# Where weight loads are issued among the batch loads of a fused RWKV-5 attention and soft-MoE kernel

## The chip, the cores and the metric

One core of one Trainium2 chip. The metric is device microseconds (us) from one execution of the whole program; the time of a kernel is the median over its runs. Engines are named as in the profile: PE is TensorE, DVE is VectorE, ACT is ScalarE, POOL is GpSimd, SP is SyncE. A "q" behind an engine (SPq) is its queue of instructions where it issues DMAs or waits. All DMAs run on the same 16 DMA engines; the profile calls the queue that POOL feeds q0 (software_dynamic), SP's q1 and ACT's q10.

## The reference

```python
# attention: batch 4, heads 8, seq 768, head_dim 48
for t in range(S):
    kt, vt, rt = (k[:, :, t], v[:, :, t], r[:, :, t])
    cur = np.einsum('bhd,bhe->bhde', u[None] * kt, vt)
    y[:, :, t] = np.einsum('bhd,bhde->bhe', rt, state + cur)
    state = w[None, :, :, None] * state + np.einsum('bhd,bhe->bhde', kt, vt)
# soft MoE on x = y as (3072, 384): E = 8 experts of 4 slots, F = 1024
logits = x @ phi                      # (3072, 32)
d = softmax over the 3072 tokens      # exp, divided by the column sums
slot_input = (d.T @ x).reshape(E, 4, 384)
slot_out[e] = np.maximum(slot_input[e] @ w1[e], 0.0) @ w2[e]
c = softmax over the 32 slots         # exp, divided by the row sums
return c @ slot_out.reshape(32, 384)  # (3072, 384)
```

r, k, v are (4, 8, 768, 48) fp32, w and u (8, 48), w1 (8, 384, 1024), w2 (8, 1024, 384). The maxima that the reference subtracts before exp are left out in the kernel, before and after the change alike.

## The kernel before

The recurrence is done in chunks of 128 time steps: six chunks a batch, 24 in all, numbered 0 to 23, so chunks 0 to 5 are batch 0, 6 to 11 batch 1, 12 to 17 batch 2 and 18 to 23 batch 3. Within a chunk, r and k are scaled by powers of the decay w (tables W_neg and w_rep, lines 104 to 106), transposed, multiplied into a masked score matrix and applied to v; between chunks the state goes on in bf16 times wm (w to the power 128, lines 107 to 114). Each finished chunk x is transposed, multiplied by phi (`lg`, line 267), exponentiated into Lexp and summed into un_p over all 24 chunks (`disp`, line 275). Only when the last chunk is in can unsiT (line 331), the slots' input, be formed.

**Stages.** A loop over i (line 303) runs chunk i's scores and outputs, the products r, k and u of chunk i + 2 (`mults`, line 157: three POOL multiplications and a cast of v on ACT, line 170), the transposes of chunk i + 1, the copy of r for chunk i + 1 (`r_copy`, line 173, on ACT) and the MoE work of chunks i - 1 and i - 2. Instructions of an engine run in the order in which they are written: the four engines' main loops are under a manual schedule, and only the code ahead of line 149 is ordered by the framework, ACT's table work (lines 102 to 107) excepted.

**Inputs.** r, k and v of a batch lie in tiles of a pool of two buffers. Batch 0 is loaded chunk by chunk (18 DMAs on SP, line 71), each further batch by three DMAs (line 66). Batch 1 is asked for right behind batch 0; batches 2 and 3 are written in `mults` one chunk into the batch before (line 161), and since there are two buffers, SP waits there until the batch that held the buffer is used up: its last user on ACT is the r copy of the batch's last chunk, which stands behind the cast of v of the next batch's first chunk.

**Weights.** w1 and w2 of the eight experts stay in SBUF as bf16. Each is fetched and cast by one DMA of POOL's queue (`load_w`, line 139), 16 in all. The list W_AT (line 289) says behind which step i of the loop each is issued, W_ORDER in which order: w1 of expert 0, w1 of 1, w2 of 0, w1 of 2, w2 of 1 and so on, the last two w2 of experts 6 and 7. In POOL's order a fetch of step i stands right behind the three products of chunk i + 2.

**MLP and output.** `up` (line 341) and `down` (line 353) run the experts on PE with the slots' four rows, in the order up 0, up 1, down 0, up 2, ..., up 7, down 6, down 7; every expert takes 24 weight loads and products for each. so_r (line 374) is the transposed result. The output loop (line 380) makes two row blocks at a time, one scaled by DVE and one by ACT, into o_s, a pool of three buffers, and writes each pair by a DMA on SP (line 393), 12 in all.

Of the kernel before, what the change touches and what calls it, by code (L numbers as in the profile page):

```python
# [11 lines left out]
def kernel(  # L12
# [18 lines left out]
    ES = moe_phi.shape[1]  # L31
# [15 lines left out]
    G = 4  # L47
    nG = nN // G

    wts = ctx.enter_context(tc.tile_pool(name="wts", bufs=1))  # L50
    w1_all = wts.tile([P, E, nM, F], bf, name="w1_all")
    w2_all = wts.tile([P, E, nF, Dm], bf, name="w2_all")
    cst = ctx.enter_context(tc.tile_pool(name="cst", bufs=1))
# [18 lines left out]
                                  in_=src[b, :, c * C:(c + 1) * C, :].rearrange("h p d -> p h d"))  # L72

    w_rep = cst.tile([P, H * D], f32, name="w_rep")
    nc.scalar.dma_start(out=w_rep[:], in_=w.flatten().partition_broadcast(P))
    w_pd = cst.tile([P, nP], f32, name="w_pd")
    nc.vector.memset(w_pd[:], 1.0)
    for par in range(2):
        nc.scalar.dma_start(out=w_pd[par * 64:par * 64 + D, :],
                            in_=w.rearrange("(q a) d -> a d q", a=2)[par])  # L80
    u_rep = cst.tile([P, H * D], f32, name="u_rep")
    nc.scalar.dma_start(out=u_rep[:], in_=u.flatten().partition_broadcast(P))
    load_batch(0)
    phi_f = cst.tile([P, nM, ES], f32, name="phi_f")
    nc.scalar.dma_start(out=phi_f[:], in_=moe_phi.rearrange("(mo p) s -> p mo s", p=P))

    ident = cst.tile([P, P], bf, name="ident")
    make_identity(nc, ident)
    mask_ut = cst.tile([P, P], f32, name="mask_ut")
    make_upper_triangular(nc, mask_ut, val=1.0, diag=False)  # L90

    iotash = cst.tile([P, 1], mybir.dt.int32, name="iotash")
    nc.gpsimd.iota(iotash, pattern=[[0, 1]], base=-C, channel_multiplier=1)
    ishf = cst.tile([P, 1], f32, name="ishf")
    nc.vector.tensor_copy(ishf[:], iotash[:])
    ishf2 = cst.tile([P, 1], f32, name="ishf2")
    nc.vector.tensor_scalar(out=ishf2[:], in0=ishf[:], scalar1=-1.0, scalar2=-1.0,
                            op0=ALU.mult, op1=ALU.add)

    logw_pd = cst.tile([P, nP], f32, name="logw_pd")  # L100
    W_neg = cst.tile([P, H, D], f32, name="W_neg")
    with tc.manual_schedule(engines={mybir.EngineType.Activation}):
        nc.scalar.activation(out=logw_pd[:], in_=w_pd[:], func=AF.Ln)
        nc.scalar.activation(out=w_rep[:], in_=w_rep[:], func=AF.Ln)
        nc.scalar.activation(out=W_neg[:].rearrange("p h d -> p (h d)"), in_=w_rep[:], func=AF.Exp, scale=ishf[:])  # L105
        nc.scalar.activation(out=w_rep[:], in_=w_rep[:], func=AF.Exp, scale=ishf2[:])
        nc.scalar.activation(out=w_pd[:], in_=logw_pd[:], func=AF.Exp, scale=float(C))

    wm = cst.tile([P, nP, D2], f32, name="wm")
    nc.vector.memset(wm[:], 0.0)  # L110
    for par in range(2):
        ps = slice(par * 64, par * 64 + 64)
        nc.vector.tensor_copy(wm[ps, :, par * D:(par + 1) * D],
                              w_pd[ps, :, None].to_broadcast([64, nP, D]))

    W_k3 = w_rep[:].rearrange("p (h d) -> p h d", h=H)
    u3 = u_rep[:].rearrange("p (h d) -> p h d", h=H)
    phi_s = cst.tile([P, nM, ES], bf, name="phi_s")
    nc.vector.tensor_copy(phi_s[:], phi_f[:])
    ones = cst.tile([P, P], bf, name="ones")  # L120
    nc.vector.memset(ones[:], 1.0)

    NB = 3
    rr_t, kk_t = [], []
# [24 lines left out]
    with tc.tile_pool(name="wk", bufs=2) as wk, \  # L149
         tc.tile_pool(name="wk3", bufs=3) as wk3, \  # L150
         tc.tile_pool(name="wk4", bufs=4) as wk4, \
         tc.tile_pool(name="ps", bufs=1, space=bass.MemoryType.PSUM) as ps, \
         tc.manual_schedule():
        un_p = ps.tile([P, nM + 1, ES], f32, name="un_p")
        st8 = {}

# [22 lines left out]
        def diag(i):  # L179
            b, c = divmod(i, nC)  # L180
            s = st8[i]
            nc.vector.tensor_mul(s["ku"][:], s["ku"][:], s["r_p"][:])  # L182
            sd_p = ps.tile([P, nP * D2 + H], f32, name="sd_p")
            s["sd"] = sd_p
            d = sd_p[:, nP * D2:nP * D2 + H]
            nc.vector.tensor_reduce(d, s["ku"][:], axis=mybir.AxisListType.X, op=ALU.add)  # L186
            dv = wk.tile([P, H, D], bf, name="dv")
            nc.vector.tensor_mul(dv[:], s["v"][:], d[:, :, None].to_broadcast([P, H, D]))  # L188
            s["dv"] = dv

        def trans(i):
            s = st8[i]
            t_p = ps.tile([P, 2, nP, P], bf, name="t_p")
            for a, nm in enumerate(("rr", "kk")):
                for q in range(nP):
                    nc.tensor.transpose(t_p[:, a, q, :],  # L196
                                        s[nm][:, 2 * q:2 * q + 2, :].rearrange("p h d -> p (h d)"), ident[:])
            t_s = wk.tile([P, 2, nP, P], bf, name="t_s")
            nc.scalar.copy(t_s[:], t_p[:])  # L199
            s["t"] = t_s  # L200
# [98 lines left out]
        r_copy(0)  # L299
        mults(1)  # L300
        diag(0)
        trans(0)
        for i in range(nN + 3):
            if i < nN:
# [19 lines left out]
            if i >= 5 and (i - 5) % G == 0:  # L324
                lexp_t((i - 5) // G)
            for n, at in enumerate(W_AT):
                if at == i:
# [6 lines left out]
    late.close()  # L334
    soT = cst.tile([P, nM, G, ES], bf, name="soT")
    with tc.tile_pool(name="ffn", bufs=2) as ffn, \
         tc.tile_pool(name="ffn_ps", bufs=2, space=bass.MemoryType.PSUM) as ffn_ps, \
         tc.manual_schedule():
        hs = {}

        def up(e):
            h_p = ffn_ps.tile([P, nF, Spe], f32, name="h_p")
            for fi in range(nF):
                for mi in range(nM):
                    nc.tensor.matmul(h_p[:, fi, :], w1_all[:, e, mi, fi * P:(fi + 1) * P],  # L345
                                     unsiT[:, mi, e * Spe:(e + 1) * Spe],
                                     start=(fi == 0 and mi == 0), stop=(fi == nF - 1 and mi == nM - 1),
                                     skip_group_check=True)
            hT = ffn.tile([P, nF, Spe], bf, name="hT")
            nc.vector.tensor_scalar_max(out=hT[:], in0=h_p[:], scalar1=0.0)  # L350
            hs[e] = hT

        def down(e):
            so_p = ffn_ps.tile([P, nM, Spe], f32, name="so_p")
            for mi in range(nM):
                for fi in range(nF):
                    nc.tensor.matmul(so_p[:, mi, :], w2_all[:, e, fi, mi * P:(mi + 1) * P], hs[e][:, fi, :],  # L357
                                     start=(fi == 0 and mi == 0), stop=(fi == nF - 1 and mi == nM - 1),
                                     skip_group_check=True)
            nc.vector.tensor_copy(soT[:, :, :, e * Spe:(e + 1) * Spe],  # L360
                                  so_p[:, :, None, :].to_broadcast([P, nM, G, Spe]))

        up(0)
        for e in range(E):
            if e + 1 < E:
                up(e + 1)
            down(e)

        so_r = cst.tile([P, Dm], bf, name="so_r")
        sr_p = ffn_ps.tile([P, Dm], bf, name="sr_p", bufs=1)  # L370
        for mi in range(nM):
            nc.tensor.transpose(sr_p[:, mi * P:(mi + 1) * P],
                                soT[:, mi, :, :].rearrange("p g s -> p (g s)"), ident[:])
        nc.vector.tensor_copy(so_r[:], sr_p[:])

    out_ap = out.rearrange("(no p) m -> p no m", p=P)
    with tc.tile_pool(name="ob", bufs=3) as ob, \
         tc.tile_pool(name="out_ps", bufs=2, space=bass.MemoryType.PSUM) as out_ps, \
         tc.manual_schedule():
        for g in range(nG):  # L380
            for jj in range(0, G, 2):
                o_s = ob.tile([P, 2, Dm], f32, name="o_s")
                for j in (jj, jj + 1):
                    o_p = out_ps.tile([P, Dm], f32, name=f"o_p{j}")
                    nc.tensor.matmul(o_p[:], LexpT[j * ES:(j + 1) * ES, g, :], so_r[j * ES:(j + 1) * ES, :],  # L385
                                     tile_position=(j * ES, 0))
                    ni = g * G + j
                    if j % 2 == 0:
                        nc.vector.tensor_scalar_mul(o_s[:, 0, :], o_p[:], rsum_r[:, ni:ni + 1])  # L389
                    else:  # L390
                        nc.scalar.activation(out=o_s[:, 1, :], in_=o_p[:], func=AF.Copy,  # L391
                                             scale=rsum_r[:, ni:ni + 1])
                nc.sync.dma_start(out=out_ap[:, g * G + jj:g * G + jj + 2, :], in_=o_s[:])
# [30 lines left out]
```

## Time and profile before

| what | value |
|---|---|
| median of 3 runs | 164.43 us (162.64 to 167.54) |
| the profiled execution | 164.1 us |
| its span, first to last instruction | 162.3 us |
| granted clock of PE, mean over the span | 0.774 of full speed |
| busy: PE, DVE, ACT, POOL | 84.6, 93.6, 77.9, 84.5 us (52, 58, 48, 52% of the span) |
| moved by DMA | 32.13 MB, mean 198 GB/s |
| of it q0 (weights), q1 (r, k, v, output), q10 (small tables) | 12.58, 18.88, 0.44 MB |

How to read it: times are us from the span's start. A timeline's row gives start, duration, engine, line and operation, and in brackets how long the engine had been idle and what it had waited for. The page's slices cut the span into 40 equal parts of 4.06 us; a digit is a busy share in tenths. In the DMA view of a stretch the slices are those of the stretch. MB are counted at the size written, so a weight's fp32 source counts half. A fetch's "us to landing" runs from its issue to its semaphore.

### The profile page before, as it was taken

To read this page: it belongs to the slowest core of one execution; us is meant where nothing else is said; L and a number is where in the kernel's file an instruction comes from. 1 tells how busy PE (TensorE), PEld (TensorE's weight loads), DVE (VectorE), ACT (ScalarE), POOL (GpSimd) and SP (SyncE) were. 2 spreads that over 40 slices of the span, in tenths; PEclk is the share of its full clock that TensorE was granted. 3 is DMA by queue.
4 is the path that set the end of the run, shared out by engine and by line. 5 is a ranking of instruction groups with operands and counts; after the bars stand their busy time and mean duration, and the time that the engine had idled before them with its cause. 6 is when DMAs were issued, how large, how long until landed. Compare 5 with 4: busy or idle time off the path is not lost.

```text
span 162.3 us, 3621 instructions
## 1 busy us (share of the span) xinstructions
PE 84.6 (52%) x1433; PEld 63.4 (39%) x1433; DVE 93.6 (58%) x198; ACT 77.9 (48%) x163; POOL 84.5 (52%) x97
## 2 busy tenths in 40 slices
PE   0004987804789874678720000077778549974400
PEld 0003665603577653456520000065556339961100
DVE  2016889904788995999930000079999822235560
ACT  0295568307668929987500000477796420005550
POOL 2019999493869997999820091079996000000000
PEclk9999999975556999999995555559999955555555
DMA  4999997999859999999999999209999992007994
GB/s 76 197 213 210 218 258 191 253 256 183 236 161 266 257 259 181 222 243 222 221 235 230 230 246 248 53 10 168 211 184 203 164 204 39 4 4 267 346 370 182
DMA packets 48593, 32.13 MB, mean 198 GB/s; under 512 B 20160, under 2 KB 45504, under 8 KB 48576
## 3 DMA queue, kind: packets, MB, share of 16 engines
q0 software_dynamic: 11520, 12.58, 47.6%
q1 hardware_dynamic: 35952, 18.88, 42.5%
q10 hardware_dynamic: 1104, 0.44, 1.6%
q8 instruction: 11, 0.18, 0.4%
q14 instruction: 6, 0.05, 0.1%
HBM read 39.77 MB, written 4.72 MB: 274 GB/s over the span
## 4 chain that ended last, share of the span: by engine, by line
DMA 31%; SPq 21%; DVE 17%; PE 16%; ACT 8%; issue 4%; ACTq 0%; DVEq 0%
DMA v_b<-in_v_dram 23%; SPq L66 12%; SPq L71 8%; DVE at_s L213 5%; DMA out_dram<-o_s 5%; PE h_p L345 3%; PE so_p L357 3%; ACT t_s L199 3%; DVE sd_p L186 3%; PE t_p L196 3%; DVE ku L182 3%; DVE dv L188 3%; DMA w_rep<-in_w_dram 3%; DVE o_s L389 2%; ACT xt_s L264 2%
## 5 line engine op out<-in xcount | busy, mean ns | idle before, releaser
L182 DVE TENSOR_TENSOR ku<-ku,r_p 128x384 f32<-128x384 f32 x24 | 13.2, 548 | 33.7 <-ACT r_p L176 32.6
L168 POOL TENSOR_TENSOR ku<-k_b,u_rep 128x384 f32<-128x384 f32 x24 | 24.0, 1002 | 14.9 <-DVE sd_p L186 14.1
L199 ACT COPY t_s<-t_p 128x1024 bf16<-128x1024 bf16 x24 | 24.3, 1011 | 15.6 <-PE t_p L196 15.6
L166 POOL TENSOR_TENSOR kk<-k_b,w_rep 128x384 bf16<-128x384 f32 x24 | 24.1, 1003 | 13.8 <-DMA k_b<-in_k_dram 11.3
L213 DVE TENSOR_TENSOR at_s<-at_p,mask_ut 128x512 bf16<-128x512 f32 x48 | 30.7, 682 | 0.0
L165 POOL TENSOR_TENSOR rr<-r_b,W_neg 128x384 bf16<-128x384 f32 x24 | 24.2, 1008 | 10.7 <-ACT W_neg L105 10.0
L170 ACT CAST v_bf<-v_b 128x384 bf16<-128x384 f32 x24 | 12.1, 506 | 33.4 <-DMA v_b<-in_v_dram 33.4
L271 PE MATMUL xl_p<-phi_s,xt_s 128*128 128x32 bf16 x72 | 5.9, 184 | 37.5 <-ACT xt_s L264 37.3
L271 PEld LDWEIGHTS <-xt_s 128*128 128x128 bf16 x72 | 3.5, 100 | 40.1 <-ACT xt_s L264 40.1
L196 PE MATMUL t_p<-ident,rr 128*128 128x128 bf16 x96 | 11.1, 249 | 12.8 <-POOL rr L165 12.8
L391 ACT ACTIVATE o_s<-o_p,rsum_r 128x384 f32<-128x384 f32 x12 | 6.8, 581 | 19.4 <-PE o_p L385 14.7
L186 DVE TENSOR_REDUCE sd_p<-ku 128x8 f32<-128x384 f32 x24 | 13.5, 561 | 0.8
L188 DVE TENSOR_TENSOR dv<-v_bf,sd_p 128x384 bf16<-128x384 bf16 x24 | 13.3, 553 | 0.8
L249 PE MATMUL y_p<-v_bf,at_s 128*128 128x48 bf16 x192 | 12.5, 192 | 2.4 <-DVE at_s L213 2.3
L264 ACT COPY xt_s<-xl_p 128x384 bf16<-128x384 bf16 x24 | 11.5, 481 | 4.1 <-PE xl_p L262 4.0
L222 PE MATMUL y_p<-dv,ident 128*128 128x384 bf16 x24 | 9.2, 383 | 6.8 <-DVE dv L188 6.6
L196 PEld LDWEIGHTS <-rr 128*128 128x128 bf16 x96 | 6.4, 108 | 15.9 <-POOL rr L165 12.8
L253 ACT CAST x_t<-y_p 128x384 bf16<-128x384 f32 x24 | 11.6, 485 | 0.3 <-PE y_p L249 0.3
L209 PE MATMUL at_p<-t_s 64*128 64x128 bf16 x192 | 11.1, 246 | 1.2 <-ACT t_s L199 1.1
L239 DVE TENSOR_TENSOR st<-sd_p,wm 128x384 bf16<-128x384 f32 x20 | 11.0, 550 | 1.2 <-PE sd_p L235 1.1
L176 ACT COPY r_p<-r_b 128x384 f32<-128x384 f32 x24 | 11.7, 488 | 0.0
L196 PE MATMUL t_p<-ident,kk 128*128 128x128 bf16 x96 | 10.9, 246 | 0.4 <-POOL kk L166 0.4
(63 smaller groups left out, 166.8 us busy)
## 6 DMA issues: line engine op xcount, KB each, us to landing
w_all<-in_moe_w_dram POOLq DMA_DIRECT2D x16, 768.0 KB, 9.5
out_dram<-o_s SPq DMA_DIRECT2D x12, 384.0 KB, 2.4
r_b<-in_r_dram SPq DMA_DIRECT2D x6, 192.0 KB, 3.6
k_b<-in_k_dram SPq DMA_DIRECT2D x6, 192.0 KB, 3.8
v_b<-in_v_dram SPq DMA_DIRECT2D x6, 192.0 KB, 3.6
w_rep<-in_w_dram ACTq DMA_DIRECT2D x1, 192.0 KB, 4.3
u_rep<-in_u_dram ACTq DMA_DIRECT2D x1, 192.0 KB, 5.3
phi_f<-in_moe_phi_dram ACTq DMA_DIRECT2D x1, 48.0 KB, 5.9
```

Of the source, the lines that this page charges most:

```text
L66: nc.sync.dma_start(out=t[:].rearrange("p h c d -> p (h c) d")[:, :, 0:D], in_=src[b].rearrange("h (c p) d -> p (h c) d", p=C))
L71: nc.sync.dma_start(out=t[:, :, c, 0:D], in_=src[b, :, c * C:(c + 1) * C, :].rearrange("h p d -> p h d"))
L165: nc.gpsimd.tensor_mul(rr[:, :, 0:D], r_b[:, :, c, 0:D], W_neg[:])
L166: nc.gpsimd.tensor_mul(kk[:, :, 0:D], k_b[:, :, c, 0:D], W_k3)
L168: nc.gpsimd.tensor_mul(ku[:], k_b[:, :, c, 0:D], u3)
L182: nc.vector.tensor_mul(s["ku"][:], s["ku"][:], s["r_p"][:])
L186: nc.vector.tensor_reduce(d, s["ku"][:], axis=mybir.AxisListType.X, op=ALU.add)
L188: nc.vector.tensor_mul(dv[:], s["v"][:], d[:, :, None].to_broadcast([P, H, D]))
L196: nc.tensor.transpose(t_p[:, a, q, :], s[nm][:, 2 * q:2 * q + 2, :].rearrange("p h d -> p (h d)"), ident[:])
L199: nc.scalar.copy(t_s[:], t_p[:])
L213: nc.vector.tensor_mul(at_s[:, a, :, :], at_p[a][:], mask_ut[:, None, :].to_broadcast([P, nP, P]))
L264: nc.scalar.copy(xt_s[:].rearrange("p m t -> p (m t)"), xl_p[:, 0:nM * P])
```

## The change

Five things change. First, W_AT: the first weight fetch moves from step 4 to step 9, the second to 10, two more stand at step 15, and twelve follow from step 16 on, two of them at steps 16 and three at step 24. Second, the whole kernel is under one manual schedule, where before the preparation (other than ACT's) was ordered by the framework. Third, the preparation: w_rep is asked for by SP ahead of the batch loads, w_pd and phi by POOL, u_rep alone by ACT; ACT loads its Ln table on a dummy value (`warm`) and then does the decay tables with nothing between; the iota for the exponents is POOL's first instruction. Fourth, w to the power 128 is made by seven squarings on DVE (`tables()`, called behind `diag(0)`) instead of Ln and Exp on ACT, and wm and phi's cast are made there as well. Fifth, the output pool has six buffers.

```diff
+    ctx.enter_context(tc.manual_schedule())
     wts = ctx.enter_context(tc.tile_pool(name="wts", bufs=1))
...
-    nc.scalar.dma_start(out=w_rep[:], in_=w.flatten().partition_broadcast(P))
-    w_pd = cst.tile([P, nP], f32, name="w_pd")
-    nc.vector.memset(w_pd[:], 1.0)
-    for par in range(2):
-        nc.scalar.dma_start(out=w_pd[par * 64:par * 64 + D, :],
-                            in_=w.rearrange("(q a) d -> a d q", a=2)[par])
+    nc.sync.dma_start(out=w_rep[:], in_=w.flatten().partition_broadcast(P))
     u_rep = cst.tile([P, H * D], f32, name="u_rep")
     nc.scalar.dma_start(out=u_rep[:], in_=u.flatten().partition_broadcast(P))
     load_batch(0)
-    phi_f = cst.tile([P, nM, ES], f32, name="phi_f")
-    nc.scalar.dma_start(out=phi_f[:], in_=moe_phi.rearrange("(mo p) s -> p mo s", p=P))
...
+    for par in range(2):
+        nc.gpsimd.dma_start(out=w_pd[par * 64:par * 64 + D, :],
+                            in_=w.rearrange("(q a) d -> a d q", a=2)[par])
+    phi_f = cst.tile([P, nM, ES], f32, name="phi_f")
+    nc.gpsimd.dma_start(out=phi_f[:], in_=moe_phi.rearrange("(mo p) s -> p mo s", p=P))
...
-    with tc.manual_schedule(engines={mybir.EngineType.Activation}):
-        nc.scalar.activation(out=logw_pd[:], in_=w_pd[:], func=AF.Ln)
-        nc.scalar.activation(out=w_rep[:], in_=w_rep[:], func=AF.Ln)
-        nc.scalar.activation(out=W_neg[:].rearrange("p h d -> p (h d)"), in_=w_rep[:], func=AF.Exp, scale=ishf[:])
-        nc.scalar.activation(out=w_rep[:], in_=w_rep[:], func=AF.Exp, scale=ishf2[:])
-        nc.scalar.activation(out=w_pd[:], in_=logw_pd[:], func=AF.Exp, scale=float(C))
+    nc.scalar.activation(out=warm[:], in_=warm[:], func=AF.Ln)
+    nc.scalar.activation(out=w_rep[:], in_=w_rep[:], func=AF.Ln)
+    nc.scalar.activation(out=W_neg[:].rearrange("p h d -> p (h d)"), in_=w_rep[:], func=AF.Exp, scale=ishf[:])
+    nc.scalar.activation(out=w_rep[:], in_=w_rep[:], func=AF.Exp, scale=ishf2[:])
...
+    def tables():
+        for _ in range(C.bit_length() - 1):
+            nc.vector.tensor_mul(w_pd[:], w_pd[:], w_pd[:])
+        for par in range(2):
+            ps = slice(par * 64, par * 64 + 64)
+            nc.vector.tensor_copy(wm[ps, :, par * D:(par + 1) * D],
+                                  w_pd[ps, :, None].to_broadcast([64, nP, D]))
+        nc.vector.tensor_copy(phi_s[:], phi_f[:])
...
-        W_AT = [4, 7, 9, 10, 11, 12, 13, 14, 15, 16, 17, 18, 19, 20, 21, 22]
+        W_AT = [9, 10, 15, 15, 16, 16, 17, 18, 19, 20, 21, 22, 23, 24, 24, 24]
...
         diag(0)
+        tables()
         trans(0)
...
-    with tc.tile_pool(name="ob", bufs=3) as ob, \
+    with tc.tile_pool(name="ob", bufs=6) as ob, \
```

On ACT, the start of the program before. w_rep and w_pd are the decay, phi_f and u_rep other constants, v_bf the cast of chunk 0's v, r_p the copy of its r.

```order
L75 DMA w_rep<-in_w_dram 128x384
L79 DMA w_pd<-in_w_dram 48x4x1 x2
L82 DMA u_rep<-in_u_dram 128x384
L85 DMA phi_f<-in_moe_phi_dram 128x3x32
L103 ACT_TABLE_LOAD
L103 ACTIVATE logw_pd<-w_pd 128x4
L104 ACTIVATE w_rep<-w_rep 128x384
L170 CAST v_bf<-v_b 128x384
L176 COPY r_p<-r_b 128x384
L105 ACT_TABLE_LOAD
L105 ACTIVATE W_neg<-w_rep,ishf 128x384
```

The same place after the change:

```order
L78 DMA u_rep<-in_u_dram 128x384
L104 ACT_TABLE_LOAD
L104 ACTIVATE warm<-warm 128x1
L105 ACTIVATE w_rep<-w_rep 128x384
L106 ACT_TABLE_LOAD
L106 ACTIVATE W_neg<-w_rep,ishf 128x384
L107 ACTIVATE w_rep<-w_rep,ishf_102 128x384
L173 CAST v_bf<-v_b 128x384
```

Four of the five DMA issues, the Ln of w_pd and the two chunk-0 instructions between the tables have gone from ahead of W_neg.

On POOL before, from the last product of chunk 16 to the products of chunk 18, batch 3's first, with a weight fetch (w_all) behind each chunk. rr, kk and ku are the three products of a chunk.

```order
L168 TENSOR_TENSOR ku<-k_b,u_rep 128x384
L142 DMA w_all<-in_moe_w_dram 128x3x1024
L165 TENSOR_TENSOR rr_140<-r_b,W_neg 128x8x48
L166 TENSOR_TENSOR kk_142<-k_b,w_rep 128x8x48
L168 TENSOR_TENSOR ku<-k_b,u_rep 128x384
L144 DMA w_all<-in_moe_w_dram 128x8x384
L165 TENSOR_TENSOR rr_132<-r_b,W_neg 128x8x48
L166 TENSOR_TENSOR kk_134<-k_b,w_rep 128x8x48
L168 TENSOR_TENSOR ku<-k_b,u_rep 128x384
L142 DMA w_all<-in_moe_w_dram 128x3x1024
```

The same engine after the change, from the end of chunk 17's products to chunk 19's first two:

```order
L169 TENSOR_TENSOR kk_138<-k_b,w_rep 128x8x48
L171 TENSOR_TENSOR ku<-k_b,u_rep 128x384
L148 DMA w_all<-in_moe_w_dram 128x8x384
L146 DMA w_all<-in_moe_w_dram 128x3x1024
L168 TENSOR_TENSOR rr_128<-r_b,W_neg 128x8x48
L169 TENSOR_TENSOR kk_130<-k_b,w_rep 128x8x48
L171 TENSOR_TENSOR ku<-k_b,u_rep 128x384
L148 DMA w_all<-in_moe_w_dram 128x8x384
L146 DMA w_all<-in_moe_w_dram 128x3x1024
L168 TENSOR_TENSOR rr_132<-r_b,W_neg 128x8x48
L169 TENSOR_TENSOR kk_134<-k_b,w_rep 128x8x48
```

Before, nine fetches stand ahead of chunk 18's products; after, four do, the last two of them directly ahead of these products, and two more stand directly behind.

## Rows read from the trace of the kernel before

**Rows 1.** The page: DMA in 40 slices, and weight queue's packets, MB, share.

```profile
DMA  4999997999859999999999999209999992007994
...
q0 software_dynamic: 11520, 12.58, 47.6%
```

**Rows 2.** The chain of waits: start, duration, what.

```profile
75.98 27.44 DMA v_b<-in_v_dram
...
133.04 0.27 DVE unsiT L331
```

**Rows 3.** Timeline of ACT, 30 to 110 us: start, duration, [idle before <-releaser].

```profile
36.64 0.51 ACT L170 CAST v_bf<-v_b 128x384 bf16<-128x384 f32 x1 [6.68 <-DMA v_b<-in_v_dram]
...
60.53 0.51 ACT L170 CAST v_bf<-v_b 128x384 bf16<-128x384 f32 x1 [2.86 <-DMA v_b<-in_v_dram]
...
103.51 0.51 ACT L170 CAST v_bf<-v_b 128x384 bf16<-128x384 f32 x1 [23.84 <-DMA v_b<-in_v_dram]
```

**Rows 4.** Timeline of SP: start, duration, DMA issued.

```profile
19.68 0.82 SPq L66 DMA_DIRECT2D r_b<-in_r_dram  x1
...
46.48 4.25 SPq L66 DMA_DIRECT2D v_b<-in_v_dram  x1
62.47 0.70 SPq L66 DMA_DIRECT2D r_b<-in_r_dram  x1
```

**Rows 5.** Timeline of POOL: weight issues, four of sixteen and the last pair.

```profile
34.13 0.93 POOL L142 DMA_DIRECT2D w_all<-in_moe_w_dram  x1
...
55.94 0.94 POOL L144 DMA_DIRECT2D w_all<-in_moe_w_dram  x1
...
79.67 0.94 POOL L144 DMA_DIRECT2D w_all<-in_moe_w_dram  x1
...
107.59 0.94 POOL L144 DMA_DIRECT2D w_all<-in_moe_w_dram  x1
...
122.63 1.82 POOL L144 DMA_DIRECT2D w_all<-in_moe_w_dram  x2
```

**Rows 6.** DMA: 92:96 (q0, q1), 110:134 (q0), 108:137 (40 slices).

```profile
q0 software_dynamic: 610, 0.47, 74.4%
q1 hardware_dynamic: 612, 0.47, 46.8%
...
q0 software_dynamic: 4715, 4.54, 120.1%
...
GB/s 0 19 58 133 201 203 204 207 214 220 203 215 215 154 140 192 197 203 211 211 205 216 212 209 124 110 173 187 174 201 220 190 198 204 203 198 94 43 12 23
```

**Rows 7.** Stretches: us, busy time of each engine, granted clock, DMA share, GB/s.

```profile
2.00:22.00 20.00, 7.08 (x65) 4.73 (x66) 8.08 (x16) 10.79 (x18) 10.24 (x11) 1.00 1.04 204
...
103.00:109.00 6.00, 3.15 (x39) 2.62 (x39) 2.87 (x5) 4.53 (x10) 2.33 (x3) 0.50 0.03 6
```

**Rows 8.** DMA issues at 26, 46, 122.6 and 123 us: KB, us to landing.

```profile
v_b<-in_v_dram SPq DMA_DIRECT2D x1, 0.2 KB, 10.0
...
v_b<-in_v_dram SPq DMA_DIRECT2D x1, 0.2 KB, 14.0
...
w_all<-in_moe_w_dram POOLq DMA_DIRECT2D x1, 768.0 KB, 9.8
...
w_all<-in_moe_w_dram POOLq DMA_DIRECT2D x2, 768.0 KB, 11.3
```

**Rows 9.** Timeline of ACT, 0 to 12 us.

```profile
7.00 1.28 ACT L103 ACT_TABLE_LOAD   x1 [7.00 <-DMA w_pd<-in_w_dram]
...
11.06 0.61 ACT L105 ACTIVATE W_neg<-w_rep,ishf 128x384 f32<-128x384 f32 x1
```

**Rows 10.** Timelines of PE and DVE at the MLP's end; DMA in 147:160.5.

```profile
141.24 0.78 PE L357 MATMUL so_p<-hT,w_all 128*128 128x4 bf16 x24
...
143.97 0.21 DVE L360 CAST soT<-so_p 128x48 bf16<-128x48 f32 x1 [0.43 <-PE so_p L357]
...
GB/s 0 314 387 410 378 419 382 410 391 387 114 419 382 360 410 400 396 396 405 232 264 410 391 351 414 391 405 391 410 159 410 396 310 410 396 401 382 423 278 0
```

More of the change, by code (lines that the diff above doesn't have):

```diff
@@ L83 @@
     load_batch(0)
-    phi_f = cst.tile([P, nM, ES], f32, name="phi_f")
-    nc.scalar.dma_start(out=phi_f[:], in_=moe_phi.rearrange("(mo p) s -> p mo s", p=P))
[L87 to L90, printed above, removed]
+    w_pd = cst.tile([P, nP], f32, name="w_pd")
+    nc.vector.memset(w_pd[:], 1.0)
+    warm = cst.tile([P, 1], f32, name="warm")
+    nc.vector.memset(warm[:], 1.0)
     iotash = cst.tile([P, 1], mybir.dt.int32, name="iotash")
@@ L98 @@
                             op0=ALU.mult, op1=ALU.add)
-    logw_pd = cst.tile([P, nP], f32, name="logw_pd")
-    W_neg = cst.tile([P, H, D], f32, name="W_neg")
-    with tc.manual_schedule(engines={mybir.EngineType.Activation}):
-        nc.scalar.activation(out=logw_pd[:], in_=w_pd[:], func=AF.Ln)
-        nc.scalar.activation(out=w_rep[:], in_=w_rep[:], func=AF.Ln)
-        nc.scalar.activation(out=W_neg[:].rearrange("p h d -> p (h d)"), in_=w_rep[:], func=AF.Exp, scale=ishf[:])
-        nc.scalar.activation(out=w_rep[:], in_=w_rep[:], func=AF.Exp, scale=ishf2[:])
-        nc.scalar.activation(out=w_pd[:], in_=logw_pd[:], func=AF.Exp, scale=float(C))
+    ident = cst.tile([P, P], bf, name="ident")
@@ new lines @@
+    make_identity(nc, ident)
+    mask_ut = cst.tile([P, P], f32, name="mask_ut")
+    make_upper_triangular(nc, mask_ut, val=1.0, diag=False)
+    for par in range(2):
[3 more added lines that the diff above has]
+    nc.gpsimd.dma_start(out=phi_f[:], in_=moe_phi.rearrange("(mo p) s -> p mo s", p=P))
+    W_neg = cst.tile([P, H, D], f32, name="W_neg")
@@ L109 @@
+    nc.scalar.activation(out=warm[:], in_=warm[:], func=AF.Ln)
+    nc.scalar.activation(out=w_rep[:], in_=w_rep[:], func=AF.Ln)
+    nc.scalar.activation(out=W_neg[:].rearrange("p h d -> p (h d)"), in_=w_rep[:], func=AF.Exp, scale=ishf[:])
+    nc.scalar.activation(out=w_rep[:], in_=w_rep[:], func=AF.Exp, scale=ishf2[:])
     wm = cst.tile([P, nP, D2], f32, name="wm")
     nc.vector.memset(wm[:], 0.0)
[L111 to L114, printed above, removed]
+    ones = cst.tile([P, P], bf, name="ones")
@@ L116 @@
+    nc.vector.memset(ones[:], 1.0)
+    phi_s = cst.tile([P, nM, ES], bf, name="phi_s")
+    def tables():
[6 more added lines that the diff above has]
+        nc.vector.tensor_copy(phi_s[:], phi_f[:])
     W_k3 = w_rep[:].rearrange("p (h d) -> p h d", h=H)
@@ L117 @@
     u3 = u_rep[:].rearrange("p (h d) -> p h d", h=H)
[L118 to L121, printed above, removed]
     NB = 3
@@ L151 @@
          tc.tile_pool(name="wk4", bufs=4) as wk4, \
-         tc.tile_pool(name="ps", bufs=1, space=bass.MemoryType.PSUM) as ps, \
-         tc.manual_schedule():
+         tc.tile_pool(name="ps", bufs=1, space=bass.MemoryType.PSUM) as ps:
         un_p = ps.tile([P, nM + 1, ES], f32, name="un_p")
@@ L336 @@
     with tc.tile_pool(name="ffn", bufs=2) as ffn, \
-         tc.tile_pool(name="ffn_ps", bufs=2, space=bass.MemoryType.PSUM) as ffn_ps, \
-         tc.manual_schedule():
+         tc.tile_pool(name="ffn_ps", bufs=2, space=bass.MemoryType.PSUM) as ffn_ps:
         hs = {}
@@ L376 @@
     out_ap = out.rearrange("(no p) m -> p no m", p=P)
-    with tc.tile_pool(name="ob", bufs=3) as ob, \
-         tc.tile_pool(name="out_ps", bufs=2, space=bass.MemoryType.PSUM) as out_ps, \
-         tc.manual_schedule():
+    with tc.tile_pool(name="ob", bufs=6) as ob, \
+         tc.tile_pool(name="out_ps", bufs=2, space=bass.MemoryType.PSUM) as out_ps:
         for g in range(nG):
```

## Prediction

> **What bounds the kernel now.** I read the page's slices first, then the chain of waits, then the timelines of ACT, SP and POOL around the place where the chain sits longest, and last the DMA view of single stretches. The profiled run took 164.1 us, its span 162.3, so 1.8 us lie around the span; the median shown is 164.43, 0.3 above that run. The DMA line stands at 9 in most slices (4.06 us each) up to the 25th and again from 109.6 to 134, with two nearly empty slices between, from 101.4 to 109.6, and three from 133.9 to 146 [rows 1]. So up to 136 us the kernel is a stream of transfers with one hole in it; after that come the MLP's last products and a write-out of some 15 us.
>
> The chain shows where compute stands still: 27.44 us on batch 3's v [rows 2]. ACT tells the same from the waiting side: its cast of that v starts at 103.51 after 23.84 us of idle time, batch 2's at 60.53 after 2.86 [rows 3]. POOL's timeline shows why the fetch is late: seven of the sixteen weight fetches are issued from 55.94 to 79.67 [rows 5], while SP asks for batch 3 only at 62.47 [rows 4]. In 92 to 96 us the two queues moved 0.47 MB each [rows 6]: batch 3 had half of the engines. While compute stands, nothing issues weights, and from 103 to 109 us the DMA engines are busy 3% of the time [rows 7]. The attention ends with the unsiT product at 133.3 [rows 2], and the MLP follows at once, since by then nearly all weights are in. The median of the last two fetches is 11.3 us from issue to landing and the earlier one took 9.8, so the last took 12.8; issued at 123.6, one 0.9 us issue after the 122.63 of the pair, it landed at 136.4 [rows 5, 8].
>
> On this the forecast turns: removing 23.84 us of stall is not worth 23.84 us. All bytes still have to come, so what the change is worth is read from when the last weight can land.
>
> **Start and tables.** W_neg was ready at 11.67 behind a table load that had waited 7.00 us for w_pd [rows 9]; that wait goes, and POOL can begin by up to 7.0 us earlier. Worth nothing: ACT sits idle for 6.68 us before batch 1's first cast at 36.64 [rows 3], and that landing is set by transfers that run full from 2 us on (busy share 1.04 [rows 7]). Without that cover it would be worth up to 7.0 us. Added are seven squarings, two copies and a cast on DVE, and three DMA issues on POOL, each at most the 0.94 us of a weight issue [rows 5], 2.8 us together, while POOL waits for W_neg anyway. SP issues w_rep ahead of r. I take 0 for all of it, bounds -0.5 and +0.5, one DMA issue either way.
>
> **Batch 2.** Three weight issues, the first at 34.13 and the last at 55.94 [rows 5], move behind its requests. Its v took 14.0 us from issue to landing; batch 1's, with no weight beside it, 10.0 [rows 8]. Issued at 46.48 [rows 4] it lands at 56.5, before ACT asks at 57.67 (60.53 less 2.86). So the wait of 2.86 us goes, and SP's request for batch 3, which waits for a copy of r that ACT makes right behind that cast, moves from 62.47 to 59.6. Bounds: 0 to 2.86. The price is that from 36.6 to about 40 us the DMA engines now have nothing to do, where they moved the first weight.
>
> **Batch 3.** Two weights run beside it, issued where the ones of 55.94 and some four us later stood. A weight is 12.58 MB / 16 = 0.786 MB; weights alone moved 4.54 MB in the 24 us from 110 to 134 [rows 6], 189 GB/s, 4.16 us each. So these two fill 57.5 to 65.8. Batch 1 took from its first issue at 19.68 [rows 4] to 36.6, 16.9 us; batch 3 from 59.6 lands at 76.5 alone, and at 79.5 if it has half of the engines until 65.8. ACT reaches its cast at 79.67 - 2.86 = 76.8, so some 3 us of the 23.84 are left. The attention then needs what it needed from 103.51 to 133.3, 29.8 us, and ends near 109.
>
> **What is late next: the weights.** Fourteen of sixteen are still to come. Two stand behind chunk 17's products, which ended where the issue at 79.67 stands [rows 5] and now end at 76.8; the others follow at one or two a chunk, and a chunk takes under 4 us (19.1 us for the six from 60.53 to 79.67), so the queue is not empty again. A weight's data comes 1.1 to 2.5 us after its issue: 107.59 the issue, above zero from 108.7, full from 110.9 in the first row of 108 to 137 [rows 5, 6]; I take 1.6. From 78.4 then: what is left of batch 3, 1.1 us, and 14 x 4.16 = 58.2 end at 137.7; the landing shows 0.4 later (136.0 and 136.4 before), 138.1. From both sides: the best slices run at some 205 GB/s, 3.84 each, last landing 133.7; with ramp and run-out six took from 108.6 to 136.0, 4.57 each, last landing 143.9. I take 4.16, the row of weights alone over the longest stretch. POOL's issues wait until the fetch eight earlier has landed, which at 4.16 us each is the case; cost 0, and one fetch (4.2 us) if it were not.
>
> **MLP and end.** Its products now run as each weight arrives and hide under the stream. After the last landing stand 24 products (0.78 us), a DVE copy (0.21) and two hand-overs, 1.1 us in all: 139.2, where soT ended at 144.18 [rows 10]. Minus 5.0.
>
> **Write-out.** With three buffers the stream has dips: 38 of 40 slices of 0.34 us hold data, 12.8 us for twelve pairs of 384 KB (4.72 MB), though between dips it runs at some 400 GB/s [rows 10]. Six buffers put twice as many in flight; at 400 it takes 11.8. Minus 1.0, bounds 0 and -1.3.
>
> Sum: 164.1 - 5.0 - 1.0 = 158.1 against the profiled run; the median is 0.3 higher, so 158.4.
>
> **Rivals.**
> A, the gain is eaten by the weights' tail. Fourteen at 4.57 land at 143.9, soT ends at 145.0: 164.1 + 0.8 - 1.0 = 163.9. For it: in 108 to 137 us single slices fall to 110 to 154 GB/s [rows 6]. Against: most of the 4.57 is the ramp at one end and the run-out at the other, and both come once.
> B, slower: DMA time left idle early that cannot be made up. If batch 3 takes 20.9 us (batch 1's 16.9 and the 4.0 by which batch 2's v was slower [rows 8]) from an unmoved 62.47, it lands at 83.4; if the weights make no headway before that and take 4.57 after it, the last lands at 147.8, soT ends at 148.9: 164.1 + 4.7 - 0 = 168.8. It decides from a last landing of about 147. For it: 36.6 to 40 us and a gap near 56 are now given away. Against: 103 to 109, empty before [rows 7], is filled.
> The Trainium skill speaks for B: "DMA: Bandwidth & Descriptors", Rules for kernel authors, has a transfer issued early, compute laid over it, and its semaphore waited for late. By that rule alone the old order is the better; this trace speaks against it in so far as early weights took half of batch 3's engines.
> C, better: weights at 3.84, last landing 133.7, soT 134.8: 164.1 - 9.4 - 1.3 = 153.4. For it: the slices at 205; against: none of the stretches holds that rate throughout.
> D, the change doesn't do what it says: batch 2 is late all the same and the stall shrinks little. That counts only if batch 3 lands after 108, since 108 + 29.8 is the forecast's last landing; otherwise it is A or B.
>
> **How the numbers follow.** Forecast 0.70, A 0.19, B with the bad part of D 0.06, C 0.05. A measurement of this kernel can tell about 2% from no change: below 161.1 is faster, above 167.7 slower. Forecast and C lie below, 0.75; A within; B above. The range leaves out C's end, B and the upper half of A: 154.0 to 163.5.
>
> **What would show it.** Right: ACT's wait for batch 3's v falls from 23.84 us to under 8; unsiT is done near 109; the DMA slices stay at 9 from 58 us to the last weight, which lands at 136 to 140; MLP products wait for transfers; the write-out has no dips. Wrong: the last weight after 143, idle DMA slices between 80 and 135, or an attention that still ends after 130.

## The result, and the profile after

| | median us | range, runs | ratio to the kernel before |
|---|---|---|---|
| before | 165.16 | 162.64 to 167.54, 4 | |
| after | 154.58 | 154.02 to 155.14, 4 | 0.9452, 95% interval 0.9339 to 0.9566 |

The kernel is 5.5% faster (4.3 to 6.6%). Executions more than 1.5% above the fastest of their kernel are left out of the ratios and stay in the medians. The forecast was 158.4 us in a range of 154.0 to 163.5; the time is 3.8 us under the forecast, 0.6 above the lower end and 1.2 above rival C (153.4). The profiled execution took 154.98 us, its span 153.2; before it was 164.1 and 162.3. The lines of the changed kernel stand two to four higher: the cast of v is L173, the fetches L146 and L148, soT L363, the output DMA L395.

The page of the kernel after, DMA and GB/s in 40 slices, now of 3.83 us each:

```profile
DMA  3999998964389929996899999999999999907994
GB/s 65 196 216 202 220 223 254 278 198 117 98 231 285 267 58 155 205 284 186 250 297 209 207 206 208 209 209 207 209 207 208 207 210 202 171 1 278 400 399 157
```

The page of the kernel before, GB/s in slices of 4.06 us:

```profile
GB/s 76 197 213 210 218 258 191 253 256 183 236 161 266 257 259 181 222 243 222 221 235 230 230 246 248 53 10 168 211 184 203 164 204 39 4 4 267 346 370 182
```

The hole at 101 to 110 us (there the 26th and 27th slice) is gone. From the 22nd to the 34th slice the weights' stream now stands at 202 to 210 GB/s; before, from the 28th to the 33rd, it went between 164 and 211. In place of the hole are two small gaps, at the 10th and 11th slice and at the 15th. The view of stretches names them; its columns are those of [rows 7]:

```profile
37.00:40.50 3.50, 1.32 (x17) 1.09 (x18) 1.61 (x4) 3.08 (x7) 0.45 (x1) 0.54 0.07 13
54.50:57.50 3.00, 2.38 (x43) 1.77 (x44) 2.93 (x7) 2.59 (x7) 2.59 (x4) 1.00 0.02 6
82.00:132.00 50.00, 31.23 (x665) 25.78 (x665) 27.06 (x64) 19.56 (x45) 23.41 (x26) 0.67 1.23 208
```

Two gaps of some 3 us with next to no transfer (13 and 6 GB/s), then 50 us at 208 GB/s without a break.

ACT's casts of the first chunk of batches 1, 2 and 3, the answer to [rows 3]:

```profile
36.91 0.51 ACT L173 CAST v_bf<-v_b 128x384 bf16<-128x384 f32 x1 [4.31 <-DMA v_b<-in_v_dram]
...
57.83 0.50 ACT L173 CAST v_bf<-v_b 128x384 bf16<-128x384 f32 x1
...
80.90 0.51 ACT L173 CAST v_bf<-v_b 128x384 bf16<-128x384 f32 x1 [2.94 <-DMA v_b<-in_v_dram]
```

The stall of 23.84 us is now 2.94, that of 2.86 is gone. SP's requests for batch 3, its DMAs for the output, and POOL's fetches two to six and the last pair, answering to [rows 4, 5]:

```profile
60.70 0.70 SPq L67 DMA_DIRECT2D r_b<-in_r_dram  x1
61.87 8.18 SPq L67 DMA_DIRECT2D k_b<-in_k_dram  x1
70.51 4.13 SPq L67 DMA_DIRECT2D v_b<-in_v_dram  x1
138.09 9.92 SPq L395 DMA_DIRECT2D out_dram<-o_s  x12
```

```profile
59.87 0.80 POOL L146 DMA_DIRECT2D w_all<-in_moe_w_dram  x1
...
76.23 0.95 POOL L148 DMA_DIRECT2D w_all<-in_moe_w_dram  x1
77.18 0.76 POOL L146 DMA_DIRECT2D w_all<-in_moe_w_dram  x1
...
80.80 0.94 POOL L148 DMA_DIRECT2D w_all<-in_moe_w_dram  x1
81.73 0.76 POOL L146 DMA_DIRECT2D w_all<-in_moe_w_dram  x1
...
103.69 1.80 POOL L148 DMA_DIRECT2D w_all<-in_moe_w_dram  x2
```

All sixteen are issued by 105.5 us (before: 124.45), so the queue holds several fetches from 82 us on. Then the MLP's end, PE's last products and DVE's unsiT and last soT, answering to [rows 2, 10]:

```profile
127.00 0.80 PE L348 MATMUL h_p<-unsiT,w_all 128*128 128x4 bf16 x24 [2.92 <-DMA w_all<-in_moe_w_dram]
130.86 0.80 PE L360 MATMUL so_p<-hT,w_all 128*128 128x4 bf16 x24 [3.06 <-DMA w_all<-in_moe_w_dram]
134.76 0.80 PE L360 MATMUL so_p<-hT,w_all 128*128 128x4 bf16 x24 [3.10 <-DMA w_all<-in_moe_w_dram]
```

```profile
110.98 0.26 DVE L335 TENSOR_TENSOR unsiT<-un_p,csum_r 128x96 bf16<-128x96 f32 x1
...
135.60 0.21 DVE L363 CAST soT<-so_p 128x48 bf16<-128x48 f32 x1 [3.69 <-PE so_p L360]
```

The attention ends 22 us sooner (unsiT at 111.2 against 133.3), yet soT only 8.4 us sooner (135.81 against 144.18): towards the end PE does 0.80 us of products and waits 3 us for the next weight, 3.86 and 3.90 us apart. The last one is in at about 134.7. Before, the MLP ran from the attention's end to soT in 10.9 us without a wait for a weight, so there the attention set the end; now the weights do. From soT to the end of the span are 17.4 us, 18.1 before; the DMA view of 138 to 153.2 us shows the write-out without a dip:

```profile
GB/s 0 0 121 376 400 392 408 392 392 408 396 416 388 392 404 396 404 408 388 392 408 400 396 408 388 400 404 400 392 408 392 392 408 340 4 0 0 0 0 22
```

So of the profiled 9.1 us, 8.4 lie ahead of soT, which now follows the last weight's landing, and 0.7 in the write-out.

### The profile page after: what moved, and what is told of

Same layout as the page of the kernel before. It is cut to its first block, busy times and chain, and to the rows that moved or that the text cites. A ratio compares the mean times of both kernels' runs of the same rounds, so it can differ in the third digit from the quotient of the medians.

```text
span 153.2 us, 3605 instructions
## 1 busy us (share of the span) xinstructions
PE 86.6 (57%) x1433; PEld 65.3 (43%) x1433; DVE 98.2 (64%) x206; ACT 77.7 (51%) x162; POOL 86.2 (56%) x100
## 4 chain that ended last, share of the span: by engine, by line
DMA 38%; SPq 21%; POOL 12%; PE 10%; ACT 6%; DVE 4%; issue 4%; ACTq 0%; DVEq 0%; POOLq 0%
DMA w_all<-in_moe_w_dram 20%; DMA v_b<-in_v_dram 14%; SPq L72 12%; SPq L67 10%; DMA out_dram<-o_s 4%; POOL rr L168 3%; PE t_p L199 3%; POOL kk L169 2%; POOL ku L171 2%; POOL w_all L148 2%; ACT t_s L202 2%; PE at_p L212 2%; ACT xt_s L267 1%; POOL w_all L146 1%; ACT r_p L179 1%
## 5 line engine op out<-in xcount | busy, mean ns | idle before, releaser
L185 DVE TENSOR_TENSOR ku<-ku,r_p 128x384 f32<-128x384 f32 x24 | 13.1, 547 | 16.3 <-POOL ku L171 8.9
L173 ACT CAST v_bf<-v_b 128x384 bf16<-128x384 f32 x24 | 12.2, 507 | 10.5 <-DMA v_b<-in_v_dram 10.5
L252 PEld LDWEIGHTS <-at_s 128*128 128x128 bf16 x192 | 8.5, 103 | 9.5 <-DVE at_s L216 8.6
L199 PE MATMUL t_p<-ident,kk 128*128 128x128 bf16 x96 | 11.5, 254 | 0.3 <-POOL kk L169 0.3
```

Of the source, the lines that this page charges most:

```text
L199: nc.tensor.transpose(t_p[:, a, q, :], s[nm][:, 2 * q:2 * q + 2, :].rearrange("p h d -> p (h d)"), ident[:])
L252: nc.tensor.matmul(y_p[:, h * D:(h + 1) * D], s["at"][:, a, q, :], s["v"][:, h, :], start=False, stop=(a == 1 and q == nP - 1), skip_group ...
```

## Experiments

All kernels compute the whole reference. Diffs of W_AT are against the changed kernel, unless another is named; a ratio is to the kernel before, run beside it, with its 95% interval. "Stall" is ACT's wait for batch 3's v (23.84 us before, 2.94 after); soT is the start of the last one (143.97 before, 135.60 after).

### The list alone, and all but the list

w_only is the kernel before with only the new list; w_old is the changed kernel with only the old list back.

```diff
-        W_AT = [9, 10, 15, 15, 16, 16, 17, 18, 19, 20, 21, 22, 23, 24, 24, 24]
+        W_AT = [4, 7, 9, 10, 11, 12, 13, 14, 15, 16, 17, 18, 19, 20, 21, 22]
```

> The kernel before with the new list of steps for the weight fetches and nothing else. Theory (the last weight's landing sets the end, and the list alone moves it): last landing near 135, write-out still with dips, 155.3 to 156.3 us. Rival (the new preparation carries part of the gain): 157.5 us or more, with batch 1 landing later than in the changed kernel.

> The changed kernel with the old list of steps: preparation and six output buffers alone. Theory: only the write-out gains, 0.7 to 1.0 us against the kernel before, so 164 to 164.5 us, with the stall on batch 3's v back at 20 us or more. Rival (preparation or the one schedule matters): 162.5 us or less.

w_only took 156.67 us, ratio 0.9488 (0.9433 to 0.9544): stall 5.39, unsiT at 113.00, soT at 136.93. It falls between the two expectations; the list carries most of the gain. w_old took 164.58 by its median, as the theory had it, but its ratio, 0.9858 (0.9779 to 0.9936), is a gain of 2.3 us, between the theory's 0.7 to 1.0 and the rival, and leaves open whether the preparation carries part. Its profile goes with the theory: the stall is back at 20.59, soT at 144.03, and only the write-out is shorter, by 0.8 us. Its page, GB/s in 40 slices of 4.04 us, has the hole at 101 to 109 us again, and behind it, where fetches are issued one a chunk, 173 to 204 GB/s:

```profile
GB/s 73 195 211 211 207 250 267 167 283 177 178 156 291 228 293 209 247 269 215 228 234 231 228 235 232 70 14 188 196 173 176 194 204 44 4 4 200 399 400 171
```

### Three output buffers

```diff
-    with tc.tile_pool(name="ob", bufs=6) as ob, \
+    with tc.tile_pool(name="ob", bufs=3) as ob, \
```

> The changed kernel with three output buffers. Theory: the dips come back in the write-out, 0.7 to 1.0 us more than the changed kernel, 155.3 to 155.6. Rival (buffers are not what made the dips): unchanged, 154.6.

155.37 us, ratio 0.9424 (0.9351 to 0.9497). The dips of [rows 10] are back, as the DMA view of 138 to 153.2 us shows, and the twelve output issues take 12.07 us on SP instead of 9.92:

```profile
GB/s 0 307 384 396 400 404 392 396 396 162 400 392 336 412 400 400 392 239 352 416 307 404 404 352 408 408 222 408 408 311 392 396 388 392 239 0 0 0 0 22
```

From soT to the end of the span are 18.3 us, 17.4 in the kernel after: in the profiles six buffers are worth 0.9 us. In the timed runs this is not shown: the medians are 0.8 us apart, but the ratios (0.9424 and 0.9452) are the other way round, and their intervals overlap.

### Fetches into the first gap, and none before step 16

first_at_4 puts one fetch where the DMA engines stood idle at 37 us; late_all keeps every weight until batch 3 is in.

```diff
-        W_AT = [9, 10, 15, 15, 16, 16, 17, 18, 19, 20, 21, 22, 23, 24, 24, 24]
+        W_AT = [4, 9, 10, 15, 15, 16, 16, 17, 18, 19, 20, 21, 22, 23, 24, 24]     # first_at_4
+        W_AT = [16, 16, 16, 16, 17, 17, 17, 17, 18, 19, 20, 21, 22, 23, 24, 24]   # late_all
```

> The changed kernel with one fetch at step 4 again, which fills the empty stretch of the DMA engines between batch 1's landing and batch 2's data (36.8 to 40.4 us in the changed kernel's trace); each later fetch moves up one place. Theory (DMA engines idle early are paid for at the end): the last landing comes one weight, 3.8 us, earlier, 150.8 us. Rival (a fetch before batch 2 delays the batches, and that is what the list was to avoid): 154.6 us or more.

> The changed kernel with all sixteen fetches behind batch 3's first products, none between the batches. Theory (idle DMA time early is paid at the end): no stall on batch 3's v, and yet the last landing is two weights later, near 142.5, 162.5 us. Rival (what helps is that nothing runs beside the batch loads): 154.6 us or less.

first_at_4 took 151.66 us, ratio 0.9163 (0.9104 to 0.9222): stall 3.43, unsiT at 112.21 (later than after), soT at 132.48, 3.1 us sooner. late_all took 164.06, ratio 0.9994 (0.9955 to 1.0033). In it batch 3 is no longer waited for at all, unsiT is at 111.05, and nothing is gained, because soT is at 145.31. Its stretches (columns as in [rows 7]) show what was given away, 4 and 7 us with next to no transfer:

```profile
36.50:40.50 4.00, 1.11 (x15) 0.88 (x16) 1.40 (x3) 3.16 (x7) 0.24 (x1) 0.65 0.03 7
55.00:62.00 7.00, 5.62 (x96) 4.13 (x95) 6.86 (x15) 5.75 (x13) 5.91 (x7) 1.00 0.00 0
```

This is rival B's mechanism, at work once too much is moved. A stall of 23.84 us removed whole is worth 0 there. Each weight not moved early is paid at the end: the two that late_all moves no longer before batch 3 is in are 2 x 3.84 = 7.7 of the 9.7 us by which its soT is later than after's (the other 2.0 are the later start of the weights' data, 81.2 us against 79.2), and the one more of first_at_4 gave 3.1 of its 3.84.

### How many fetches are waiting

> The changed kernel with one fetch at step 15 and one at each step from 16 to 23, the last five behind step 24, so that from 78 to about 100 us one or two fetches are queued where the changed kernel has two to five. Theory (the 189 GB/s of the kernel before in 110 to 134 us came from too short a queue, the 205 of the changed kernel from fetches that wait ready): 185 to 197 GB/s in 84 to 100 us, last landing 1 to 2.5 us later, 155.5 to 157 us. Rival (the rate is what it is with one fetch running, and the pauses of before came from something else): 203 to 207 GB/s there and 154.6 us.

```diff
-        W_AT = [9, 10, 15, 15, 16, 16, 17, 18, 19, 20, 21, 22, 23, 24, 24, 24]
+        W_AT = [9, 10, 15, 16, 17, 18, 19, 20, 21, 22, 23, 24, 24, 24, 24, 24]
```

single took 158.14 us, ratio 0.9664 (0.9586 to 0.9742), soT at 137.97. The DMA view of 84 to 107 us, 40 slices, first of single (one fetch a chunk), then of the kernel after:

```profile
GB/s 214 207 214 214 235 175 126 189 196 198 200 199 213 213 200 214 199 221 207 163 154 183 176 190 199 214 157 173 182 202 207 214 203 182 128 153 167 205 188 184
DMA packets 3902, 4.40 MB, mean 191 GB/s; under 512 B 81, under 2 KB 2788, under 8 KB 3898
```

```profile
GB/s 220 210 207 214 236 184 196 197 208 202 206 207 212 216 221 203 210 219 200 195 203 203 210 200 228 197 213 212 228 199 214 212 193 203 203 212 202 201 216 208
DMA packets 4321, 4.78 MB, mean 208 GB/s; under 512 B 94, under 2 KB 3153, under 8 KB 4317
q0 software_dynamic: 4317, 4.73, 121.3%
```

The same stretch: 191 against 208 GB/s. With one fetch a chunk the stream sags to 126 to 160 again and again, as in 110 to 134 before [rows 6]; with more waiting it doesn't. The packets of q0 show where the sags stand: at the change from one fetch to the next, when the next was issued late. Of the 14 changes in single, before and w_old at which the next fetch had been issued 2.4 to 4.1 us ahead, ten fall below 165 GB/s (over 0.6 us). Of the 59 changes in these three and in after, shifted, first_at_4 and ob3 with 5.4 us or more, none falls below 175. The pace of issuing alone does not explain it: the fetches of before from 107.59 to 122.63 and those of after from 85.35 to 100.38 came 3.76 us apart alike, enough for 209 GB/s, and ran at 189 with little ahead of them and at 206 behind others (q0's row). In single it has a part: 4.11 us apart from 79.92 to 100.47, its fetches could bring no more than 191. Once its last eight are issued, single's stream too runs at 207 (110 to 132 us). The rate came as expected; soT came 2.4 us later, inside the 1 to 2.5 expected, while the medians lie 3.5 apart, more than expected.

### Filling both gaps

```diff
-        W_AT = [9, 10, 15, 15, 16, 16, 17, 18, 19, 20, 21, 22, 23, 24, 24, 24]
+        W_AT = [4, 8, 9, 10, 15, 15, 16, 16, 17, 18, 19, 20, 21, 22, 23, 24]
```

> The changed kernel with fetches at steps 4, 8, 9 and 10, two each at 15 and 16, and one a step after that. Theory (only the last landing counts, and the attention, done at 111 us, has some 20 us to spare): the stall on batch 3's v grows to 6 to 10 us, the attention ends at 115 to 119, and the time still falls below that of one fetch at step 4, to 148.5 to 150 us. Rival (more fetches between the batches take back the gain through that stall): 151.7 us or more.

A miss: 155.19 us, ratio 0.948 (0.9383 to 0.9577). The stall grew to 15.11 us, and POOL, which issues the fetches, stood at chunk 19's ku, behind which the next fetch is written:

```profile
92.62 0.51 ACT L173 CAST v_bf<-v_b 128x384 bf16<-128x384 f32 x1 [15.11 <-DMA v_b<-in_v_dram]
```

```profile
95.76 1.00 POOL L171 TENSOR_TENSOR ku<-k_b,u_rep 128x384 f32<-128x384 f32 x1 [11.76 <-DVE sd_p L189]
```

The queue ran low meanwhile (142 GB/s in the page's slice from 95.6 to 99.4 us). Three fetches instead of two ran beside batches 2 and 3. SP's issue of batch 3's k, 4.99 us long in late_all with no fetch beside it and 8.18 after, took 10.56 here and lasted until 71.97 instead of 70.05; v was asked for from 72.42 to 76.84. What goes with 2 us becoming 12 of stall is told below.

The theory left out a term: the end is the later of the last landing and the attention's end plus the MLP. unsiT was done at 122.40, PE then made the products with no wait for a weight, and soT ended at 135.47, 13.1 us on. The weights were late as well, since their last packets ended at 132.5, 1.2 us after those of first_at_4, where one fetch more ahead should bring them sooner. The time that the attention can spare is the 20 us of the expectation less the MLP.

### One fetch fewer beside the batches

```diff
-        W_AT = [9, 10, 15, 15, 16, 16, 17, 18, 19, 20, 21, 22, 23, 24, 24, 24]
+        W_AT = [4, 8, 9, 15, 15, 16, 16, 17, 18, 19, 20, 21, 22, 23, 24, 24]
```

> The changed kernel with its first three fetches at steps 4, 8 and 9, then two each at 15 and 16 and one a step. Theory (idle DMA time is paid at the end, as long as the batches land in time and the queue holds two or more): the gap near 56 us closes as well, batch 3's v lands within 3 us of where one fetch at step 4 left it, last landing near 129, 149.0 to 150.5 us. Rival (a fetch beside batch 2's end delays batch 3 and the queue runs dry behind it, as with four fetches between the batches): 151.7 us or more.

149.12 us (148.91 to 150.07, 6 runs), ratio 0.9082 (0.9052 to 0.9112), as expected, and below both kernels. Both gaps are filled, the stall is 0.65, soT at 130.68. Its stretches, columns as in [rows 7]:

```profile
37.00:40.50 3.50, 1.22 (x16) 0.99 (x17) 1.51 (x3) 3.17 (x7) 0.43 (x2) 0.71 1.07 201
54.50:57.50 3.00, 2.57 (x44) 1.95 (x44) 2.93 (x6) 2.66 (x7) 3.00 (x4) 1.00 1.12 203
```

### The preparation

no_prep is the kernel before with the new list and six buffers; after_5 is the changed kernel once more on the same chip, both in five rounds.

> The kernel before with the new list of steps and six output buffers, the preparation as it was. The changed kernel runs beside it on the same chip. Theory (the preparation is hidden behind batch 1's load): within 0.7 us of the changed kernel, 154.6 to 155.3. Rival (the preparation carries a part, as the 1.3 us between the list alone and the changed kernel with three buffers suggest): 1.0 to 1.8 us above it.

> The changed kernel as it is, for the comparison on one chip: 154.6 us by both.

no_prep took 156.45 us (154.74 to 159.92), ratio 0.9513 (0.9476 to 0.955); after_5 155.34 (154.14 to 156.89), ratio 0.9421 (0.9378 to 0.9463). The intervals just fail to meet (0.9476 and 0.9463): the preparation, the one schedule and `tables()` together, which no run separates, are worth 1.1 us by the medians and 1.5 by the ratios. no_prep's profiled execution was its fastest, with soT at 135.45, and shows no loss. no_prep_again and no_prep_third are two more profiled executions of it.

> The kernel before with the new list and six output buffers, preparation as before, profiled once more: its first profiled execution was its fastest (154.74 us against a median of 156.45), so what makes the median slower than that of the changed kernel (155.34) was not in it. Theory: the old preparation delays the start; an execution of 156 us or more then has batch 1's first cast after 37.4 (36.40 in the fast one), and unsiT later than 110.8 by as much. Rival: the start is the same within 0.5 us and the loss is in the stream of weights, with the last soT later than the start accounts for and slices under 205 GB/s from 85 us on. Third: a time near 154.7 again says nothing.

> The same kernel and the same expectations as in the run beside it: a second execution to read, since executions of this kernel have stretched from 154.7 to 159.9 us. Theory (the start): batch 1's first cast after 37.4 in an execution of 156 us or more. Rival (the stream): cast within 0.5 us of 36.4, and the loss between the last cast of v and the last soT.

no_prep_third took 155.01 us and reads like the first. no_prep_again took 160.21; its mean clock, 0.783, is not lower than the others' (0.775 and 0.764). Batch 1's cast is at 36.43: the start did not slip. Nor was the stream slower by itself; it sags only behind the stall. What slipped is batch 3's v, which neither expectation had named:

```profile
91.56 0.51 ACT L170 CAST v_bf<-v_b 128x384 bf16<-128x384 f32 x1 [15.31 <-DMA v_b<-in_v_dram]
```

```profile
70.96 5.12 SPq L66 DMA_DIRECT2D v_b<-in_v_dram  x1
```

```profile
75.23 0.94 POOL L144 DMA_DIRECT2D w_all<-in_moe_w_dram  x1
```

SP finished issuing v at 76.08, 0.85 us after POOL had begun the fetch behind chunk 17's products. In 81 to 82 us the two queues (packets, MB) ran like this, and beside it the kernel after in 77 to 78, its weight issued at 76.23 as well:

```profile
q0 software_dynamic: 152, 0.12, 74.1%
q1 hardware_dynamic: 152, 0.12, 46.5%
```

```profile
q1 hardware_dynamic: 425, 0.33, 108.1%
```

Read so, the profiles fall in two groups. The margin is the start of that fetch less the end of v's issue:

| kernel | margin us | stall us |
|---|---|---|
| shifted | 3.50 | 0.65 |
| after | 1.59 | 2.94 |
| single | 1.54 | 2.99 |
| ob3 | 1.48 | 3.06 |
| first_at_4 | 1.16 | 3.43 |
| after_5 (156.58 us) | 1.00 | 4.61 |
| no_prep_third | 0.87 | 3.71 |
| no_prep | 0.63 | 3.78 |
| w_only | -0.10 | 5.39 |
| no_prep_again | -0.85 | 15.31 |
| filled | -1.06 | 15.11 |

In the nine profiles with a margin of -0.10 or more v's data come first and have the engines alone; in the two with -0.85 and -1.06 the weights' come first, and v gets half. The number of fetches is not what decides: no_prep, no_prep_third and no_prep_again are one kernel. Nor does the stall follow the margin strictly, as after_5 shows. filled's stall belongs to the second group. In the profiles the new preparation, with this list, has margins of 1.59 and 1.00 where the old one has 0.87, 0.63 and -0.85, so it may make that case rarer: two of no_prep's eight executions took 160 us, none of the changed kernel's ten over 156.9. That the 159.92 among the timed ones was such a case is not shown, and the middle ones of no_prep's times, 155.7 to 156.9, are not explained by it. No run changed the margin alone.

## Why the prediction was right, and where a size was off

**The turn of the argument held.** 20.9 of 23.84 us of stall went and the time fell by 9: what counted was the last weight's landing, with most of the MLP hidden under the stream. late_all is the plain proof. One reading on the way was wrong and carries nothing: POOL did issue a fetch while compute stood still, at 95.25 us.

**Batch 2, right; its consequence 1.1 us late.** The wait of 2.86 us went. SP's request for batch 3 came at 60.70, not 59.6, since the copy of r that frees the buffer now stood behind a copy of t_s that waited for PE.

**Batch 3, right.** Forecast: landing at 79.5, 3 us of stall left, attention done near 109. Measured: landing at 80.8, 2.94, 111.2.

**The weights: the term that was mis-sized.** The step put 14 fetches at 4.16 us, from 110 to 134 of before, and the last landing at 138.1; it took place at 134.7. In 84 to 107 us q0 moved 4.73 MB, 206 GB/s or 3.82 us a fetch, and the last products stand 3.86 and 3.90 apart. That is the lower bound that the step had given (3.84 at 205 GB/s), and rival C's. At 3.84 the price is 14 x 0.32 = 4.5 us too high. The other 1.1 us of the difference of 3.4 go the other way and lie at the stream's two ends: the weights' data moved beside the last of v from 79.2 and had the engines alone from 80.4 only (forecast 79.5), and the rest stands behind the last fetch. So what ran is C's mechanism, to which the forecast gave a chance of 0.05; that the time lies inside the range, by 0.6 us, is owed in part to those 1.1 us, which the forecast did not have, and is luck to that extent. What failed was the choice of the longest row as the nearest. In that stretch POOL had issued one fetch a chunk, so few were waiting; the change issues the first four behind batch 3 in two pairs, so that from then on several wait. single and w_old show that the slower rate comes back with the old way of issuing. The argument that no stretch held 205 throughout was true, and said nothing on a fuller queue.

**MLP and end, right.** From the landing to soT's end 1.1 us; the last four of the sixteen sets of products waited for their weight, the twelve before ran one behind the other.

**Write-out, right in kind.** Forecast -1.0, profile -0.7; the timed runs do not tell six buffers from three.

**Start and tables: too small.** Taken as 0 within 0.5; timed, 1.1 to 1.5. The forecast's cover was there: POOL began at 8.26 instead of 11.76, and batch 1's cast came at 36.91, no sooner than before. What the step did not look at is when SP's and POOL's issues for batch 3 fall, 40 us further on; whether the 1.1 us come from there is open, since two of no_prep's three profiles show no loss.

**The signs.** Two did not come: the last weight landed at 134.7, not at 136 to 140, and the DMA digits fall to 6 and 8 once more after 58 us, in the 19th and 20th slice (69 to 76.6).

**Rivals.** B did not decide at this list, though the gaps it named are real: filling them is worth another 5.6 us (0.9421 to 0.9082, on one chip). The Trainium skill, "DMA: Bandwidth & Descriptors", Rules for kernel authors, would have a transfer issued early. The runs here show both sides of it: fetches into empty stretches gained 5.6 us, and fetches that came into a load that compute waits for went with a stall of 15 us.

## What to carry to other kernels

When a fixed number of bytes must pass before the end, price a removed stall by the later of two ends, the last landing and the compute that has still to follow (10.9 to 13.1 us of MLP here), and price that landing at the rate that the queue will have after the change, not at the one it has in a stretch where the change also alters how many transfers are waiting. Put prefetches into the stretches in which nothing else is outstanding, and issue the first one behind a critical load only when that load has been issued whole: here a margin of 0.6 us or more went with stalls under 5 us in every profile, one of -0.85 with 15. Keep the issuing engine's fetches off places where it waits for compute that itself waits for data.

## What the runs showed of the hardware

The rate of the weights' queue depends on how far ahead the next fetch is issued: 191 GB/s in 84 to 107 us with one issued a chunk, 208 with several waiting, for transfers of the same form. The loss stands at the change from one fetch to the next, where the next was issued 4.1 us or less ahead (ten of 14 such changes), and is absent at 5.4 us or more (59 changes).

Two queues that both have packets share the engines by packets and not by bytes (152 and 152 in 81 to 82 us of no_prep_again, 0.12 MB each; in 86 to 87, 80 and 80, with 0.16 and 0.06 MB). This is what the Trainium skill says, "DMA: Bandwidth & Descriptors", Queues, rings and completion order: each engine goes round the queues that have work. By it alone a fetch should take its share while the load still runs. In the kernel after, the fetch of 76.23 moved nothing before 79 us, while v, whose last packets ended at 80.4, went on at 326 GB/s in 77 to 78; in no_prep_again the one of 75.23 was moving in 76 to 77. No run here shows what holds it back; which of the two was issued first goes along with it in ten of the eleven profiles of the table, and w_only stands at the edge.
